# A linear-attention and MLP block on one core: layer-norm moments by a power on GpSimd, and five operand pairs prepared in the sweep

## The chip, the cores and the metric

The kernel runs on one core of a Trainium2 chip. The metric is the device time of one launch in microseconds (us). Three runs of the kernel before took 1133.1, 1133.49 and 1134.76 us, median 1133.49.

The engines are named as in the profile: PE is TensorE (PEld its weight loads), DVE is VectorE, ACT is ScalarE, POOL is GpSimd and SP the queue that issues DMAs. Each engine works through its own instructions in program order and waits for the others by semaphores.

## The reference

The input x has 2048 rows of 576 values. Two branches read it and a gate mixes them (shortened):

```python
qkv = (x @ wqkv)                        # 32 heads of 18
phi = lambda t: where(t > 0, t + 1, exp(t)) + 1e-6
kv  = einsum("bhsd,bhse->bhde", phi(k), v)
z   = phi(k).sum(over rows)
a   = (phi(q) @ kv) / (phi(q) @ z + 1e-6) @ wo

y = (x - mean(x)) / sqrt(var(x) + 1e-5)     # per row
b = gelu(y @ w1 + b1) @ w2 + b2             # 576 -> 4608 -> 576

g = sigmoid((x * gate_w).sum(-1))
out = g * a + (1 - g) * b
```

Everything is float32. To reach that accuracy a product is made of several matmuls over operands that are split into a rounded high part and the rest (a "split": ACT copies into the high part, DVE subtracts).

## The kernel before, in words

The 2048 rows are 16 tiles of 128. They are taken in pairs: `ORDER` lists the tiles so that neighbours in it form a pair, and `PLACE` is a tile's position in that list. Pairs 0 to 3 belong to the first half of the rows (`sup` 0), pairs 4 to 7 to the second.

**The sweep** (the loop `for n in range(FIRST, NT)`, after three tiles that are written out) visits each tile once. PE projects keys (`project(i, KEY, half)`, two halves of 14 matmuls), adds the first part of the products of the tile before (`add_products(before, 0)`), projects queries (two halves), and adds the second part. The projections use PSUM banks 6 and 7 in turn, so each half overwrites a bank that was read two halves earlier. The reader is `phi`: ACT makes e = exp of the negative part, then DVE combines it with the bank (`k<-ps,e` for keys, `accs<-ps,e` or `acc<-ps,e` for queries). DVE also makes the rest parts: `ks` of the keys, `xs` of the rows of x (twice, 512 and 64 wide), and `y<-t,y` of the next tile's transposed x (twice). POOL sums the keys over the tiles (`pks<-pks,k`). The last three tiles have no queries in the loop; these follow later.

**Jobs.** Into each tile of the sweep other work is put at three places, its thirds: `run(3 * n)` after the splits of keys and rows, `run(3 * n + 1)` after the queries' phi, `run(3 * n + 2)` after the second part of the products. `at(n, f, ...)` enters a job under its number. All jobs run in the program order of their engines; nothing is rescheduled.

**Moments and gates.** ACT takes each tile's sum of squares (`moments_of`) and copies the row sums out of the projection (`sums_of_x`). Groups of 2, 2, 4 and 8 tiles (`MOMENTS`) then go through `gates_in`, `gates_act` and `gates_out`: eleven DVE operations and, on ACT, an exponential and a square root, each with its own table of functions, which ACT reloads. `share_moments` transposes the group's means and inverse deviations by PE through bank 6, copies them out and stores them to DRAM as rows. The last group is done in the attention, after the sweep.

**Pairs for the MLP.** The MLP's first product uses a scheme with seven operands made of the four blocks of a pair (B11, B21, B12, B22) and four differences (T1 to T4; B12 has T1's place). `load_pair` loads `rows` (the pair's moments, spread over all partitions) and the transposed x into `yr`; `normal_pair` adds the negative mean and multiplies by the inverse deviation, once for each tile of the pair (4 operations, 768 wide); `sum_pair` makes the differences (4 operations, 384 wide); `split_pair` and `split_tails` split them in four parts (`ys`, the last in a place within `y`), and `store_pair` puts them to DRAM (`yd`). `rows` and `yr` lie in `spare`, a piece of the big tile `accs` (so does much else: in the profile "accs<-accs 128x768" are the additions and products of a pair and "accs<-accs 128x384" its differences). All of this is DVE's before, but for the copies of the splits. Pairs 0 to 3 are prepared in the sweep at hand-written thirds, pairs 4 to 7 in the first passes of the MLP, by `after(...)`.

**After the sweep** come the state kv and its product with `wo` (`xk`, `kvs`, `project_values`), the attention over 16 tiles, then the MLP from about 265 us to the end.

Of the kernel before, what the change touches and what calls it, by code (L numbers as in the profile page):

```python
# [33 lines left out]
MOMENTS = ((0, 2), (2, 4), (4, 8), (8, 16))  # L34
# [77 lines left out]
def tile_gated_mix(ctx: ExitStack, tc: tile.TileContext, x, xm, xe, wm, we, wvm, wve, wo, um, ue, w2, b1, b2, gw, out):  # L112
# [54 lines left out]
    nmean = keep.tile([P, NT], F32, name="nmean")  # L167
# [4 lines left out]
    mr = [keep.tile([P, 2, q1 - q0], F32, name=f"mr{b}") for b, (q0, q1) in enumerate(MOMENTS)]  # L172
    mt = keep.tile([P, 2, NT], F32, name="mt")
    mrt = keep.tile([2 * max(q1 - q0 for q0, q1 in MOMENTS), P], F32, name="mrt")
    moments = [dram.tile([2, (q1 - q0) * P], F32, name=f"moments{b}") for b, (q0, q1) in enumerate(MOMENTS)]
# [72 lines left out]

    def moments_of(i):
        own = slice(PLACE[i], PLACE[i] + 1)  # L250
        act.activation(xnraw[i], xnraw[i], AF.Square, bias=nmean[:, own], accum_out=sumsq[:, own])
# [30 lines left out]
    def sums_of_x(i):  # L282
        own = slice(PLACE[i], PLACE[i] + 1)
        act.activation(gsum[:, own], banks[i, KEY, 1][:, HALF:HALF + 1], AF.Copy)
        act.activation(nmean[:, own], banks[i, KEY, 1][:, HALF + 1:HALF + 2], AF.Copy, scale=-1 / D)
# [59 lines left out]
    def gate_parts(b):  # L345
        q0, q1 = MOMENTS[b]
        own, n = slice(q0, q1), q1 - q0
        return own, mt[:, 0, :n], mt[:, 1, :n], mr[b][:, 1]

    def gates_in(b):  # L350
        own, ve, _, _ = gate_parts(b)
        dve.tensor_copy(mr[b][:, 0], nmean[:, own])
        dve.tensor_scalar(ve, sumsq[:, own], 1 / D, EPS_LN, op0=OP.mult, op1=OP.add)

        dve.tensor_scalar(g[:, own], gsum[:, own], -87.0, None, op0=OP.max)

    def gates_act(b):
        own, ve, _, rstd = gate_parts(b)
        act.activation(g[:, own], g[:, own], AF.Exp, scale=-1.0)
        act.activation(rstd, ve, AF.Sqrt)  # L360
        if MOMENTS[b][1] < NT:
            act.activation(tiny, ones[:, 0:1], AF.Exp)

    def gates_out(b):
        own, ve, vr, rstd = gate_parts(b)
# [3 lines left out]
        dve.reciprocal(rstd, rstd)  # L369
# [19 lines left out]
    def load_pair(sup, j):  # L389
        q = sup * TPS + 2 * j  # L390
        b = [q0 <= q < q1 for q0, q1 in MOMENTS].index(True)
        c0 = (q - MOMENTS[b][0]) * P
        sp.dma_start(rows, moments[b][None, :, c0:c0 + 2 * P].to_broadcast([P, 2, 2 * P]))
        for a, m in enumerate((B11, B12)):
            i = ORDER[q + a]
            own = yr[:, m:m + 2]
            sp.dma_start(own[:, :, 0:2].rearrange("p h t n -> p h (t n)"), xm[i].rearrange("p (h n) -> p h n", h=2))
            for h in range(2):
                sp.dma_start(own[:, h, 2], four_times(xe[i], h))

    def normal_pair(sup, j, a, k):
        m = (B11, B12)[a]
        own = yr[:, m:m + 2].rearrange("p m s n -> p (m s) n")
        row = rows[:, k:k + 1, a * P:(a + 1) * P].to_broadcast([P, 6, P])
        dve.tensor_tensor(out=own, in0=own, in1=row, op=(OP.add, OP.mult)[k])

    def sum_pair(sup, j, n):
        to, x0, x1 = ((T3, B22, B12), (T1, B12, B11), (T2, B22, T1), (T4, B21, T2))[n]
        dve.tensor_tensor(out=yr[:, to], in0=yr[:, x0], in1=yr[:, x1], op=OP.subtract)
# [198 lines left out]
    ysc.close()  # L608
    a2 = ExitStack()
# [30 lines left out]
    xk = spare[:, :5 * D].rearrange("p (t n) -> p t n", n=D)  # L640
# [21 lines left out]
    project(late[1], QUERY, 1, n=0)  # L662
    kv = [ps[:GW, 1 + j // 3, j % 3 * GW:(j % 3 + 1) * GW] for j in range(G)]
# [252 lines left out]
    for j in range(4):  # L916
# [300 lines left out]
```

## Time and profile before

| | |
|---|---|
| runs | 1133.1, 1133.49, 1134.76 us |
| span of the profiled execution | 1130.0 us |
| the runs' median less that span | 3.5 us |
| PE busy | 1114.3 us, 99% |
| PEld, DVE, ACT, POOL busy | 90%, 76%, 49%, 27% |
| granted TensorE clock | 1.000 |

The profile holds one execution, with a span of 1130.0 us from its first to its last instruction; what lies around the span isn't in it, and the difference to the runs' median is the only measure of it here. All instructions have the line L108, since a helper (`InOrder`) issues them; they are told apart by tile and shape. In a row "out<-in" names the tiles, then come shapes and the count; a bracket at the end of a row of the time line is the engine's idle time before it, and what ended it.

### The profile page before, as it was taken

The page shows a single profiled execution, that of the slowest core. Times are in us where ns is not written, and L with a number is a line of the kernel's source. Part 1 is how long each engine was busy: PE and PEld are TensorE (multiplying, and loading weights), DVE is VectorE, ACT ScalarE, POOL GpSimd, SP SyncE. Part 2 cuts the span into 40 slices and gives each one's busy share as a digit, 9 for nine tenths or more (in the row PEclk, how much of TensorE's full clock was granted, in tenths as well). Part 3 has the DMA queues.
Part 4 walks back from the last instruction along what each step waited for, and adds up shares of the span by engine and source line. Part 5 has one row for each costly group of instructions (what it writes and reads, how often), then busy time and mean ns, then how long its engine had stood idle before and what let it go on. Part 6 is the DMA issues. An engine that isn't in the chain of part 4 may idle for free.

```text
span 1130.0 us, 18099 instructions
## 1 busy us (share of the span) xinstructions
PE 1114.3 (99%) x6871; PEld 1021.4 (90%) x6871; DVE 862.6 (76%) x1292; ACT 556.4 (49%) x953; POOL 303.3 (27%) x247
## 2 busy tenths in 40 slices
PE   8999899999999999999999999999999999999998
PEld 8999899999899999999999999989999999899988
DVE  4567675896569878779768775578898889888985
ACT  6667665453554544544444543364444444454441
POOL 1011112342111113112123111234353435343520
PEclk9999999999999999999999999999999999999999
DMA  6237555524554763654764549844444444444452
GB/s 177 63 113 259 164 174 186 201 94 161 182 169 142 250 223 137 232 168 168 240 212 154 210 142 388 308 121 131 126 127 136 126 126 128 136 124 126 131 180 84
DMA packets 102860, 189.84 MB, mean 168 GB/s; under 512 B 8159, under 2 KB 58623, under 8 KB 98550
## 3 DMA queue, kind: packets, MB, share of 16 engines
q1 hardware_dynamic: 102210, 188.10, 50.7%
q8 instruction: 54, 0.88, 0.3%
q10 hardware_dynamic: 564, 0.59, 0.2%
q14 instruction: 32, 0.26, 0.1%
HBM read 121.93 MB, written 66.73 MB: 167 GB/s over the span
## 4 chain that ended last, share of the span: by engine, by line
PE 89%; DVE 6%; ACT 2%; issue 1%; DMA 1%; SPq 0%; ACTq 0%; DVEq 0%
PE ps L108 89%; DVE den L108 1%; DVE accs L108 1%; DVE qt L108 1%; DVE region L108 1%; DVE u L108 0%; DVE acc L108 0%; DMA s<-in_wm 0%; DVE y L108 0%; DMA s<-in_we 0%; ACT L108 0%; SPq L108 0%; ACT h L108 0%; ACT u L108 0%; DVE wp L108 0%
## 5 line engine op out<-in xcount | busy, mean ns | idle before, releaser
L108 PEld LDWEIGHTS ps<-region,h 128*128 128x128 f32 x2568 | 368.5, 188 | 22.7 <-DVE accs L108 1.0
L108 PE MATMUL ps<-region,h 128*128 128x288 f32 x2568 | 383.1, 295 | 0.5 <-DVE region L108 0.2
L108 PE MATMUL ps<-y,wa 128*128 128x512 f32 x1008 | 265.0, 392 | 0.0
L108 POOL TENSOR_TENSOR fresh<-fresh 128x384 f32<-128x384 f32 (+1 forms) x128 | 137.8, 1081 | 439.5 <-DMA w1d<-wb 198.6
L108 PE MATMUL ps<-y,wb 128*128 128x512 f32 x756 | 200.9, 394 | 1.0 <-ACT u L108 1.0
L108 PEld LDWEIGHTS ps<-y,wa 128*128 128x128 f32 x1008 | 177.8, 188 | 26.2
L108 DVE TENSOR_TENSOR accs<-ps,accs 128x576 f32<-128x576 f32 x210 | 158.0, 753 | 33.2 <-PE ps L108 23.5
L108 ACT ACTIVATE h<-u,b1s 128x512 fp32r<-128x512 f32 x90 | 65.3, 725 | 214.8 <-DVE u L108 214.8
L108 PEld LDWEIGHTS ps<-y,wb 128*128 128x128 f32 x756 | 132.9, 188 | 23.0 <-ACT u L108 1.7
L108 DVE SCALAR_TENSOR_TENSOR accs<-ps,omg,accs 128x576 f32<-128x576 f32 (+1 forms) x146 | 118.0, 809 | 43.1 <-PE ps L108 42.3
L108 ACT ACTIVATE u<-ps 128x512 f32<-128x512 f32 x108 | 63.8, 591 | 149.9 <-PE ps L108 149.6
L108 POOL TENSOR_TENSOR u<-u 128x512 f32<-128x512 f32 x64 | 100.3, 1567 | 125.3 <-ACT u L108 121.6
L108 PE MATMUL ps<-y 128*128 128x288 f32 (+1 forms) x896 | 126.7, 298 | 1.1 <-ACT y L108 0.6
L108 PEld LDWEIGHTS ps<-y 128*128 128x128 f32 x896 | 123.5, 190 | 3.3 <-ACT y L108 1.2
L108 DVE TENSOR_TENSOR h<-u,h 128x512 fp32r<-128x512 f32 x142 | 104.8, 738 | 27.3 <-ACT u L108 27.1
L108 ACT ACTIVATE u<-u,b1s 128x512 f32<-128x512 f32 x108 | 78.2, 724 | 53.9 <-DVE u L108 50.9
L108 DVE TENSOR_TENSOR u<-ps,u 128x512 f32<-128x512 f32 x108 | 74.1, 686 | 36.6 <-ACT u L108 23.4
L108 PEld LDWEIGHTS ps<-region 128*128 128x128 f32 x600 | 90.3, 188 | 8.9 <-ACT accs L108 0.5
L108 DVE TENSOR_TENSOR region<-fresh,region 128x576 fp32r<-128x576 f32 (+1 forms) x83 | 81.2, 978 | 20.5 <-ACT region L108 20.5
L108 PE MATMUL ps<-region 128*128 128x288 f32 x600 | 96.2, 295 | 0.1
L108 PE MATMUL ps<-wp,qt 128*128 128x288 f32 x448 | 63.6, 298 | 0.8 <-DVE qt L108 0.8
L108 PEld LDWEIGHTS ps<-wp,qt 128*128 128x128 f32 x448 | 59.9, 188 | 1.3 <-DVE qt L108 1.3
(134 smaller groups left out, 1047.0 us busy)
## 6 DMA issues: line engine op xcount, KB each, us to landing
w1d<-wa SPq DMA_DIRECT2D x18, 1280.0 KB
wa<-w1d SPq DMA_DIRECT2D x72, 320.0 KB
y<-yd SPq DMA_DIRECT2D x14, 1280.0 KB
w1d<-wb SPq DMA_DIRECT2D x18, 960.0 KB
wb<-w1d SPq DMA_DIRECT2D x54, 320.0 KB
fresh<-in_w SPq DMA_DIRECT2D x20, 576.0 KB
fresh<-in_w SPq DMA_DIRECT2D x32, 288.0 KB
fresh<-in_um SPq DMA_DIRECT2D x64, 128.0 KB
```

The lines of the kernel that those rows point to most:

```text
L108: return lambda *args, **kwargs: self.tc.keep_in_program_order(op(*args, **kwargs))
```

## The change

- The mean (negative) is written by ACT straight into `mr`, a tile with the moments of all pairs; the inverse deviation is the power -0.5 of the variance, taken on POOL pair by pair (`scale_in`), followed by the same Newton step on DVE (`scale_out`).
- `share_moments` stores a pair's moments from `mr` without a transpose: 128 partitions x 4 single values.
- Gates keep only the sigmoid, in two groups of eight tiles, the second right after the sweep.
- Five pairs, not four, are prepared in the sweep, one every six thirds of a tile. In each, the additions of the mean and the four differences are POOL's; products and splits stay with DVE and ACT. `load_pair` issues `rows` last.
- The fifth pair is dropped from the MLP's first passes. `xk` gets a place of its own, and the list of jobs goes on behind the loop.

On POOL the sweep's order before, two tiles of a pair and more (`pks` is the sum of the keys):

```order
L108 TENSOR_TENSOR pks<-pks,k 128x576 x2
L108 MEMSET kvs 126x1152
L108 TENSOR_TENSOR pks<-pks,k 128x576 x13
L108 TENSOR_TENSOR qz<-accs,pks 128x576 x8
L108 TENSOR_TENSOR qz<-acc_87,pks 128x576
```

and after the change, from the third tile's sum on (`mr<-mt` is the power):

```order
L110 TENSOR_TENSOR pks<-pks,k 128x576
L110 TENSOR_TENSOR mr<-mt,minus_half 128x2
L110 TENSOR_TENSOR pks<-pks,k 128x576
L110 TENSOR_TENSOR accs<-accs 128x768 x2
L110 TENSOR_TENSOR accs<-accs 128x384 x4
L110 TENSOR_TENSOR pks<-pks,k 128x576
```

Between two sums of keys POOL now has, in every second tile, a pair's two additions and four differences.

On DVE, in the sweep, before: a pair's four additions and products, with the next tile behind them, where the differences begin.

```order
L108 TENSOR_TENSOR accs<-accs 128x768 x4
L108 SCALAR_TENSOR_TENSOR k<-ps,e 128x288
L108 TENSOR_TENSOR y<-t,y 128x512
L108 TENSOR_TENSOR y<-t,y 64x128
L108 SCALAR_TENSOR_TENSOR k<-ps,e 128x288
L108 SCALAR_TENSOR_TENSOR ks<-k,ks 128x576
L108 TENSOR_TENSOR xs<-xn,xs 128x512
L108 TENSOR_TENSOR xs<-xn,xs 128x64
L108 TENSOR_TENSOR accs<-accs 128x384 x2
L108 TENSOR_TENSOR ys_543<-accs,ys_543 128x2x256
```

After, the tile in which a pair is normalized:

```order
L110 SCALAR_TENSOR_TENSOR ks<-k,ks 128x576
L110 TENSOR_TENSOR xs<-xn,xs 128x512
L110 TENSOR_TENSOR xs<-xn,xs 128x64
L110 TENSOR_TENSOR y<-accs,y 128x256
L110 SCALAR_TENSOR_TENSOR y<-y,low_rows,accs 128x128
L110 SCALAR_TENSOR_TENSOR accs<-ps,e 128x288 x2
L110 TENSOR_TENSOR accs<-accs 128x768 x2
L110 TENSOR_TENSOR ys_544<-accs,ys_544 128x2x256
L110 SCALAR_TENSOR_TENSOR ys_544<-ys_544,low_rows,accs 128x2x128
L110 SCALAR_TENSOR_TENSOR k<-ps,e 128x288
```

Two 768-wide operations instead of four stand behind the phi of the queries (`accs<-ps,e`), and none of 384; the last split of the pair before (`y<-accs,y`, called T4 below) stands ahead of these phi.

The diff, cut to its core:

```diff
-    nmean = keep.tile([P, NT], F32, name="nmean")
+    mr = keep.tile([P, NP, 2, 2], F32, name="mr")
...
+    minus_half = keep.tile([P, 2], F32, name="minus_half")
+    dve.memset(minus_half, -0.5)
+    moments = [dram.tile([2, 2 * P], F32, name=f"moments{q}") for q in range(NP)]
...
     def gates_act(b):
-        own, ve, _, rstd = gate_parts(b)
+        own = slice(*GATES[b])
         act.activation(g[:, own], g[:, own], AF.Exp, scale=-1.0)
-        act.activation(rstd, ve, AF.Sqrt)
-        if MOMENTS[b][1] < NT:
-            act.activation(tiny, ones[:, 0:1], AF.Exp)
...
+    def scale_in(q):
+        ve = mt[:, 0]
+        dve.tensor_scalar(ve, sumsq[:, 2 * q:2 * q + 2], 1 / D, EPS_LN, op0=OP.mult, op1=OP.add)
+        pool.tensor_tensor(out=mr[:, q, 1], in0=ve, in1=minus_half, op=OP.pow)
+
+    def scale_out(q):
+        ve, vr, r = mt[:, 0], mt[:, 1], mr[:, q, 1]
 
-        dve.tensor_mul(vr, rstd, rstd)
+        dve.tensor_mul(vr, r, r)
         dve.tensor_mul(vr, vr, ve)
         dve.tensor_scalar(vr, vr, -0.5, 1.5, op0=OP.mult, op1=OP.add)
-        dve.tensor_mul(rstd, rstd, vr)
-
-    def share_moments(b, p):
-
-        n = 2 * (MOMENTS[b][1] - MOMENTS[b][0])
-        pe.transpose(p[:n], mr[b].rearrange("p a t -> p (a t)"), ident)
-        act.activation(mrt[:n], p[:n], AF.Copy)
-        sp.dma_start(moments[b].rearrange("a (t n) -> (a t) n", n=P), mrt[:n])
+        dve.tensor_mul(r, r, vr)
+
+    def share_moments(q):
+        sp.dma_start(moments[q].rearrange("a (t n) -> n a t", n=P), mr[:, q])
...
-    def normal_pair(sup, j, a, k):
+    def normal_pair(sup, j, a, k, by=dve):
...
-    def sum_pair(sup, j, n):
+    def sum_pair(sup, j, n, by=dve):
...
-    for b, (n, shared) in enumerate(((9, 13), (13, 16), (24, 28))):
-        at(n, gates_in, b)
-        at(n + 1, gates_act, b)
-        at(n + 2, gates_out, b)
-        at(shared, share_moments, b, ps[:, 6, :P])
-
-    for j, (loaded, *parts) in enumerate(((13, 18, 19, 20, 21), (20, 25, 27, 28, 29), (28, 33, 34, 35, 36),
-                                          (35, 41, 42, 44, 45))):
...
+    def prepare_scale(q, n):
+        at(n, scale_in, q)
+        at(n + 1, scale_out, q)
+        at(n + 2, share_moments, q)
+
+    for q in range(PAIRS_IN_SWEEP):
+        sup, j = divmod(q, TPB)
+        n = 6 * q
+        prepare_scale(q, max(n + 7, 3 * FIRST))
+        at(n + 13, load_pair, sup, j)
         for a in range(2):
-            for k in range(2):
-                at(loaded + 3 + a, normal_pair, 0, j, a, k)
+            at(n + 15, normal_pair, sup, j, a, 0, pool)
+            at(n + 16, normal_pair, sup, j, a, 1)
         for m in range(4):
-            at(parts[m // 2], sum_pair, 0, j, m)
...
+            at(n + 17, sum_pair, sup, j, m, pool)
+        for part in range(4):
+            at(n + (17, 19, 20, 21)[part], split_pair, sup, j, part, lambda part=part: y_stages[part])
+            at(n + (17, 19, 20, 21)[part], split_tails, sup, j, part)
+            at(n + (20, 22, 23, 24)[part], store_pair, sup, j, part)
+    prepare_scale(5, 37)
+    prepare_scale(6, 44)
+    for n, f in ((49, gates_in), (50, gates_act), (51, gates_out)):
+        at(n, f, 1)
+    prepare_scale(NP - 1, 50)
...
-    xk = spare[:, :5 * D].rearrange("p (t n) -> p t n", n=D)
+    xk = xkp.tile([P, 5, D], F32, name="xk")
...
-    for i, part in ((1, gates_in), (2, gates_act), (3, gates_out)):
-        extra[i] += [lambda part=part: part(len(MOMENTS) - 1)]
-    extra[5] += [lambda: share_moments(len(MOMENTS) - 1, two_of(t_pairs)[:, 0, :P])]
...
-    for j in range(4):
+    for j in range(PAIRS_IN_SWEEP - TPB, TPB):
         k, s = divmod(15 + 28 * j, TPS)
```

More of the change, by code (lines that the diff above doesn't have):

```diff
@@ L33 @@
 PLACE = [ORDER.index(i) for i in range(NT)]
-MOMENTS = ((0, 2), (2, 4), (4, 8), (8, 16))
+NP = NT // 2
+GATES = ((0, 8), (8, 16))
+PAIRS_IN_SWEEP = 5
 EPS_PHI = 1e-6
@@ L171, in tile_gated_mix @@
     omg = keep.tile([P, NT], F32, name="omg")
[L172 to L175, printed above, removed]
+    mt = keep.tile([P, 2, 2], F32, name="mt")
+    minus_half = keep.tile([P, 2], F32, name="minus_half")
+    dve.memset(minus_half, -0.5)
+    moments = [dram.tile([2, 2 * P], F32, name=f"moments{q}") for q in range(NP)]
     w1d = [dram.tile([P, 7, 5, P], F32, name=f"w1d{c}") for c in range(NCHUNK)]
@@ L247, in load_xn, with nmean_of @@
         sp.dma_start(xnraw[i], x[i * P:(i + 1) * P, :])
+    def nmean_of(i):
+        q, a = divmod(PLACE[i], 2)
+        return mr[:, q, 0, a:a + 1]
     def moments_of(i):
         own = slice(PLACE[i], PLACE[i] + 1)
-        act.activation(xnraw[i], xnraw[i], AF.Square, bias=nmean[:, own], accum_out=sumsq[:, own])
+        act.activation(xnraw[i], xnraw[i], AF.Square, bias=nmean_of(i), accum_out=sumsq[:, own])
     halves_in, banks = cycle((6, 7)), {}
@@ L284, in sums_of_x @@
         act.activation(gsum[:, own], banks[i, KEY, 1][:, HALF:HALF + 1], AF.Copy)
-        act.activation(nmean[:, own], banks[i, KEY, 1][:, HALF + 1:HALF + 2], AF.Copy, scale=-1 / D)
+        act.activation(nmean_of(i), banks[i, KEY, 1][:, HALF + 1:HALF + 2], AF.Copy, scale=-1 / D)
     def sum_keys(i):
@@ L343, in add_products @@
                 pe.matmul(to, a, b, start=opens and i == ORDER[0], stop=i == ORDER[-1], skip_group_check=True)
[L345 to L348, printed above, removed]
     def gates_in(b):
-        own, ve, _, _ = gate_parts(b)
-        dve.tensor_copy(mr[b][:, 0], nmean[:, own])
-        dve.tensor_scalar(ve, sumsq[:, own], 1 / D, EPS_LN, op0=OP.mult, op1=OP.add)
+        own = slice(*GATES[b])
         dve.tensor_scalar(g[:, own], gsum[:, own], -87.0, None, op0=OP.max)
     def gates_act(b):
-        own, ve, _, rstd = gate_parts(b)
+        own = slice(*GATES[b])
         act.activation(g[:, own], g[:, own], AF.Exp, scale=-1.0)
-        act.activation(rstd, ve, AF.Sqrt)
-        if MOMENTS[b][1] < NT:
-            act.activation(tiny, ones[:, 0:1], AF.Exp)
     def gates_out(b):
-        own, ve, vr, rstd = gate_parts(b)
+        own = slice(*GATES[b])
         dve.tensor_scalar(g[:, own], g[:, own], 1.0, None, op0=OP.add)
@@ L390, in load_pair @@
         q = sup * TPS + 2 * j
-        b = [q0 <= q < q1 for q0, q1 in MOMENTS].index(True)
-        c0 = (q - MOMENTS[b][0]) * P
-        sp.dma_start(rows, moments[b][None, :, c0:c0 + 2 * P].to_broadcast([P, 2, 2 * P]))
         for a, m in enumerate((B11, B12)):
@@ L399, in load_pair @@
                 sp.dma_start(own[:, h, 2], four_times(xe[i], h))
-    def normal_pair(sup, j, a, k):
+        sp.dma_start(rows, moments[q // 2][None].to_broadcast([P, 2, 2 * P]))
+    def normal_pair(sup, j, a, k, by=dve):
         m = (B11, B12)[a]
@@ L404, in normal_pair @@
         row = rows[:, k:k + 1, a * P:(a + 1) * P].to_broadcast([P, 6, P])
-        dve.tensor_tensor(out=own, in0=own, in1=row, op=(OP.add, OP.mult)[k])
-    def sum_pair(sup, j, n):
+        by.tensor_tensor(out=own, in0=own, in1=row, op=(OP.add, OP.mult)[k])
+    def sum_pair(sup, j, n, by=dve):
         to, x0, x1 = ((T3, B22, B12), (T1, B12, B11), (T2, B22, T1), (T4, B21, T2))[n]
-        dve.tensor_tensor(out=yr[:, to], in0=yr[:, x0], in1=yr[:, x1], op=OP.subtract)
+        by.tensor_tensor(out=yr[:, to], in0=yr[:, x0], in1=yr[:, x1], op=OP.subtract)
     ys = {}
@@ L531, in tile_gated_mix @@
     y_stages.append(y_place.rearrange("p (m s n) -> p m s n", m=2, s=5))
-    jobs = {n: [] for n in range(3 * NT)}
+    jobs = {n: [] for n in range(3 * NT + 9)}
     def at(n, f, *args):
@@ L601, in tile_gated_mix @@
     moments_of(end)
+    run(48)
     for part in range(2):
         add_products(end, part)
+    run(49)
     pz = [ps[:, 6 + half, :HALF] for half in range(2)]
@@ L662, in tile_gated_mix @@
     project(late[1], QUERY, 1, n=0)
+    run(50)
     kv = [ps[:GW, 1 + j // 3, j % 3 * GW:(j % 3 + 1) * GW] for j in range(G)]
@@ L668, in tile_gated_mix @@
     queries_out(late[1])
+    run(51)
     for i in range(1, 3):
@@ L704, in tile_gated_mix @@
         project_values(t)
+        run(52 + t)
         if t < 4:
```

13 lines of the change are left out of this document (5 added, 8 removed).

## The prediction, made before the result was known

> **What bounds the kernel now.** I read the page first, then the busy time by stretch, then the time line of the sweep, because almost everything that the change moves lies in the sweep (about 20 to 185 us).
>
> ```profile
> span 1130.0 us, 18099 instructions
> PE 1114.3 (99%) x6871; PEld 1021.4 (90%) x6871; DVE 862.6 (76%) x1292; ACT 556.4 (49%) x953; POOL 303.3 (27%) x247
> ```
>
> TensorE (PE) is the bound: it is idle for 15.7 us in all. The three runs have a median of 1133.49 us, 3.5 us over this span; I keep that distance and count changes of the span. The stretches tell where PE is idle (each row: length, then the busy us of PE, PEld, DVE, ACT, POOL).
>
> ```profile
> 50.00:75.00 25.00, 23.80 (x159) 22.55 (x158) 14.17 (x40) 18.95 (x43) 2.87 (x2) 1.00 0.29 81
> 100.00:125.00 25.00, 22.02 (x146) 20.57 (x145) 18.17 (x43) 17.56 (x40) 2.87 (x2) 1.00 0.45 146
> 125.00:150.00 25.00, 25.00 (x170) 24.07 (x169) 18.93 (x34) 16.26 (x37) 2.88 (x2) 1.00 0.61 194
> 210.00:265.00 55.00, 53.41 (x407) 52.20 (x406) 51.02 (x91) 26.24 (x58) 20.11 (x15) 1.00 0.54 200
> 300.00:725.00 425.00, 425.00 (x2575) 388.01 (x2574) 319.88 (x424) 196.60 (x262) 84.90 (x68) 1.00 0.61 210
> ```
>
> From 300 to 725 us PE never stops, so that a pair less for the VectorE (DVE) there can give nothing. What can be won is 25.00 - 23.80 = 1.20, 25.00 - 22.02 = 2.98 and 55.00 - 53.41 = 1.59 us. The first two are the transposes of the moments, as the time line shows, and part of the third is:
>
> ```profile
> 73.02 0.27 PE L108 MATMUL ps<-accs,mr 128*4 128x128 f32 x1 [1.20 <-DVE accs L108]
> 121.35 0.27 PE L108 MATMUL ps<-accs,mr 128*8 128x128 f32 x1 [2.78 <-DVE acc L108]
> 237.83 0.66 PE L108 MATMUL ps<-accs 128*128 128x128 f32 x4 [0.65 <-DVE qt L108]
> ```
>
> The transpose borrows bank 6, so PE stands until DVE has finished the phi (`queries_out`) that reads this bank, and DVE is late there because of the gates' small operations.
>
> **What the change removes.** Four transposes with these waits, four copies out of PSUM, seven reloads of ScalarE's (ACT's) function tables, and in the attention, where DVE is busy for 51.02 of 55 us, eleven small DVE operations.
>
> ```profile
> L108 ACT ACT_TABLE_LOAD x9 | 11.5, 1283 | 4.4 <-DMA t<-in_xm 4.4
> L108 DVE TENSOR_TENSOR mr<-mr,mt x4: 160/162/168, 52.7 to 232.5; 128x2 f32<-128x2 f32 x2, 128x4 f32<-128x4 f32 x1, 128x8 f32<-128x8 f32 x1
> L108 SPq DMA_DIRECT2D moments<-mrt x4: 276/317/340, 61.6 to 238.3; - x4
> ```
>
> ACT is no bound (49%), so its 7 x 1.28 us by themselves are worth nothing. Eleven operations of 0.16 us are 1.8 us of DVE in the attention; PE's idle 1.59 us there can shrink by most of it, I take 1.4. Sum won: 1.20 + 2.98 + 1.4 = **5.6 us**; bounds 4.2 (the transposes alone) and 5.8.
>
> **What it adds at no cost.** Eight powers of 128x2 on GpSimd (POOL): the trace has no power. Below, nothing; above, an operation of POOL's longest shape here (2.8 us, quoted below), which the lighter tile of each two could still carry (its room is worked out below): zero. The eight stores of moments have 512 runs of 4 bytes instead of 4 to 16 rows; the queue's issue was 0.32 us, at most a few times that. Nothing waits for it for four thirds of a tile, so I count zero. The second gate group and the last power land between 185 and 195 us, some nine small operations (1.5 us); the product kvs at 195.57 (quoted below with the tile) is preceded by 1.92 us of idle DVE. Zero too.
>
> **What it moves, and the lock.** Per pair, two of four 768-wide operations and all four 384-wide ones go from DVE to POOL:
>
> ```profile
> L108 DVE TENSOR_TENSOR accs<-accs 128x768 f32<-128x768 f32 x16 | 15.1, 953 | 0.3
> L108 DVE TENSOR_TENSOR accs<-accs 128x384 f32<-128x384 f32 x16 | 8.8, 553 | 0.3
> L108 POOL TENSOR_TENSOR accs<-accs 128x384 f32<-128x384 f32 x8 | 8.8, 1113 | 10.4 <-DMA accs<-in_ue 6.3 <-DMA b2b<-in_b 3.8
> L108 POOL TENSOR_TENSOR accs<-accs 128x1152 f32<-128x1152 f32 x3 | 8.4, 2803 | 20.6 <-DVE accs L108 20.6
> ```
>
> DVE is freed of 2 x 0.95 + 4 x 0.55 = 4.1 us. On POOL a 384-wide one takes 1.0 to 1.1 us and a 768-wide one, halfway to 1152, some 1.9: 2 x 1.9 + 4 x 1.05 = 8 us per pair. POOL has the time (2.9 of 25 us busy). But DVE and POOL shut each other out. Two rows of each engine:
>
> ```profile
> 20.77 0.76 DVE L108 SCALAR_TENSOR_TENSOR ks<-k,ks 128x576 fp32r<-128x576 f32 x1
> 20.98 1.86 POOL L108 TENSOR_TENSOR pks<-pks,k 128x576 f32<-128x576 f32 x1 [2.90 <-DVE k L108]
> 21.67 0.46 DVE L108 SCALAR_TENSOR_TENSOR k<-ps,e 128x288 f32<-128x288 f32 x1
> 129.03 1.44 POOL L108 TENSOR_TENSOR pks<-pks,k 128x576 f32<-128x576 f32 x1 [11.51 <-DVE k L108]
> 129.85 1.24 DVE L108 SCALAR_TENSOR_TENSOR ks<-k,ks 128x576 fp32r<-128x576 f32 x1 [0.96 <-ACT ks L108]
> ```
>
> At 20.77 DVE began first: its ks took 0.76 us and POOL's sum was stretched from 1.44 to 1.86. At 129.85 POOL was first and DVE took 1.24: 129.85 + 1.24 - 0.76 = 130.33, so it began work 0.14 us before POOL's end at 130.47. That is a wait for the whole instruction of the other, not a sharing. The phi, with one operand in PSUM, takes 0.46 us under POOL's sum at 21.67 as it does alone at 131.92 (below), so only DVE operations with two SBUF operands are shut out. The Trainium skill (SBUF — State Buffer, "SBUF: two separate sides") has the same: a port pair of DVE and GpSimd held by whoever started first for the whole instruction. The trace agrees, 1.24 against 0.76 us. Neither says who goes next when POOL waits and DVE has a second such operation right behind the first; on that the sign hangs.
>
> Now one undisturbed tile of the sweep, with the deadlines of PE:
>
> ```profile
> 131.01 0.81 DVE L108 TENSOR_TENSOR xs<-xn,xs 128x512 fp32r<-128x512 f32 x2
> 131.92 0.46 DVE L108 SCALAR_TENSOR_TENSOR acc<-ps,e 128x288 f32<-128x288 f32 x1
> 133.77 0.46 DVE L108 SCALAR_TENSOR_TENSOR acc<-ps,e 128x288 f32<-128x288 f32 x1 [1.39 <-ACT e L108]
> 134.65 3.90 PE L108 MATMUL ps<-y 128*128 128x288 f32 x28
> 137.87 0.45 DVE L108 SCALAR_TENSOR_TENSOR k<-ps,e 128x288 f32<-128x288 f32 x1
> 140.14 3.87 PE L108 MATMUL ps<-y 128*128 128x288 f32 x28
> 145.85 3.90 PE L108 MATMUL ps<-y 128*128 128x288 f32 x28
> 157.05 3.90 PE L108 MATMUL ps<-y 128*128 128x288 f32 x28
> 172.01 3.90 PE L108 MATMUL ps<-y 128*128 128x288 f32 x28
> 195.57 0.81 DVE L108 TENSOR_TENSOR kvs<-ps,accs 126x126 f32<-126x126 f32 x5 [1.92 <-PE ps L108]
> ```
>
> A tile is 145.85 - 134.65 = 11.2 us of PE. The next tile's keys at 134.65 overwrite the bank of the first query half, so the phi of 131.92 must be over by then; its slack is 134.65 - 132.38 = 2.3 us. The phi of 137.87 has until 140.14.
>
> In the new order POOL has, behind the sum of the keys (pks), the two additions of a pair at once; DVE has ks, xs twice, the last piece of the pair before (T4), the two phi, the two products. Other durations needed:
>
> ```profile
> L108 DVE TENSOR_TENSOR xs<-xn,xs 128x512 fp32r<-128x512 f32 x16 | 10.9, 681 | 0.1
> L108 DVE TENSOR_TENSOR xs<-xn,xs 128x64 fp32r<-128x64 f32 x16 | 3.4, 212 | 0.0
> L108 DVE TENSOR_TENSOR y<-accs,y 128x256 fp32r<-128x256 f32 x4 | 1.7, 413 | 0.0
> L108 DVE SCALAR_TENSOR_TENSOR y<-y,low_rows,accs 128x128 fp32r<-128x128 f32 x4 | 1.4, 340 | 0.0
> L108 DVE TENSOR_TENSOR ys<-accs,ys 128x512 fp32r<-128x512 f32 x12 | 8.2, 686 | 3.0 <-ACT ys L108 3.0
> L108 DVE SCALAR_TENSOR_TENSOR ys<-ys,low_rows,accs 128x256 fp32r<-128x256 f32 x12 | 5.7, 479 | 0.0
> L108 DVE TENSOR_TENSOR y<-t,y 128x512 fp32r<-128x512 f32 x13 | 9.0, 691 | 1.1 <-ACT y L108 0.2
> L108 DVE TENSOR_TENSOR y<-t,y 64x128 fp32r<-64x128 f32 x13 | 3.8, 289 | 0.4
> ```
>
> If the two engines take turns: ks ends at 131.09; POOL's first addition follows, to 132.9; xs 132.76 to 133.44; the second addition to 135.2; the short xs 135.06 to 135.27; T4 0.41 + 0.34, to 136.0; phi 136.0 to 136.45. PE starts its keys at 136.45 instead of 134.65: 1.8 us lost. Behind it the four subtractions on POOL take turns with ys, its tail and the two y, and the phi of the second key half comes another 0.2 us late. **2.0 us a pair** for pairs 1 to 3. A check from the sums: DVE's own work in this tile is 0.76 + 0.89 + 0.75 + 0.92 + 1.9 + 1.17 + 0.92 + 0.98 = 8.3 us, its waits 0.5 (pks) + 2 x 1.76 (additions) + about 3 (subtractions, 4 x 0.91 less what the phi cover), together 15.3. The other tile of each two has two splits (2.3) and five small operations (0.8) in place of T4, products and ys, 7.6 us, 8.1 with the wait for pks, so 3.1 us of room. 15.3 + 8.1 - 22.4 = 1.0 us cannot be made good however the slack is used: the lower bound of a pair. The upper one, when `rows` lands some 3 us late and the products wait for it, is 2.7. Pair 0 has no T4 before it: 136.45 - 0.75 - 134.65 = 1.05. Pair 4 falls into the last tiles, which have no queries and last half of 172.01 - 157.05 = 14.96, 7.5 us each; the same waits there push the split of the last tile's x behind the keys at 172.01, where I get 3.0 us (bounds 1.7 and 4). Sum lost: 1.05 + 3 x 2.0 + 3.0 = **10.0 us**; bounds 1.05 + 3 x 1.0 + 1.7 = 5.8 and 1.05 + 3 x 2.7 + 4 = 13.2.
>
> Taking turns it is 10.0 - 5.6 = +4.4 us: 1133.5 + 4.4 = **1138**. Its own range is 1133.5 + 5.8 - 5.8 = 1133.5 to 1133.5 + 13.2 - 4.2 = 1142.
>
> **Rivals.** (1) DVE keeps the port while it has operations queued. Then xs, xs and T4 run on behind ks to 132.7, the additions overlap both phi, the first product starts at 134.5 and the second, behind the second addition, at 137.2; the phi of the keys ends at 139.9, before 140.14. No stall is left, the 5.6 us are won whole: 1128. For it: DVE's operations follow each other without a gap (0.68 + 0.21 took 0.81 us at 131.01), which leaves POOL little time to get in. Against it: nowhere in the trace does POOL wait at such a pair, so nothing shows it. (2) Mixed: POOL gets in at some of the borders, and half of the 10 us is lost: 5.0 - 5.6, that is 1133, no change. (3) The change doesn't win what its removals promise, because PE's waits at 73 and 121 us come from DVE's lateness and return at the next matmul of bank 6, while turns are taken: of the 4.2 us some 2 return, 1140. Speaks against it that DVE loses the gates' operations too. Taking turns costs from the point at which POOL holds the port for more than 2.3 us between ks and the first phi; (1) decides as soon as the second xs goes ahead of POOL's second addition.
>
> **How the numbers follow.** Turns 0.44, DVE keeps the port 0.33, mixed 0.18, waits that return 0.05. A measurement of this kernel tells a change from none at about 0.2%, 2.3 us. Of the turns' 0.44 some 0.04 lies at their lower bound, within it. Slower: 0.40 + 0.05 = 0.45; within: 0.18 + 0.04 = 0.22; faster: 0.33. Predicted time 1138, that of the likeliest. The range from 1127 (all of 5.8 us and a little) to 1142 holds the turns with their bounds and the other cases.
>
> **What would show it.** The phi of the queries, in tiles with the additions, ends 3 to 4 us after its matmuls instead of 1.4; PE's idle time before the keys names DVE, about 2 us every second tile from 70 to 165 us, and PE is busy for 23 of 25 us there; POOL's additions take 1.9 us, more where DVE was first; xs takes about 1.8 us from its start. Wrong it is if PE is busy for 25 of 25 us in these stretches, or if POOL's additions are stretched to 3 us and xs isn't: then DVE kept the port, and the time is 1128.

## The result, and the profile after

The changed kernel takes 1141.05 us (median of four runs, 1139.73 to 1142.28) against 1133.3 us before on the same chip: 1.0066 times as long, 95% interval 1.0052 to 1.0080. It is slower by 7.5 us (5.9 to 9.1), as forecast in sign; the forecast size was 4.4.

The head of the page after, and the stretches (length, busy us of PE, PEld, DVE, ACT, POOL, then clock, DMA share, GB/s):

```profile
span 1138.3 us, 18127 instructions
PE 1116.6 (98%) x6867; PEld 1023.5 (90%) x6867; DVE 866.7 (76%) x1267; ACT 545.7 (48%) x933; POOL 354.9 (31%) x285
50.00:75.00 25.00, 25.00 (x170) 24.06 (x169) 14.95 (x30) 12.79 (x31) 7.22 (x5) 1.00 0.52 105
75.00:100.00 25.00, 23.68 (x160) 22.46 (x159) 22.13 (x36) 16.16 (x38) 13.96 (x10) 1.00 0.64 183
100.00:125.00 25.00, 25.00 (x166) 23.62 (x164) 18.91 (x36) 13.86 (x33) 12.53 (x11) 1.00 0.92 236
125.00:150.00 25.00, 18.23 (x111) 17.54 (x111) 14.27 (x27) 14.76 (x34) 9.84 (x8) 0.86 0.84 186
150.00:192.00 42.00, 38.36 (x242) 35.32 (x241) 37.13 (x59) 24.79 (x58) 23.00 (x17) 1.00 0.80 182
217.00:272.00 55.00, 54.49 (x420) 53.93 (x419) 48.98 (x81) 25.98 (x58) 20.89 (x16) 1.00 0.61 236
```

The gains are there: PE is busy for 25.00 us at 50 and at 100 us, where it lost 1.20 and 2.98, and its idle time in the attention went from 1.59 to 0.51. The losses are there too, in three places; the one at 125 us, 25.00 - 18.23 = 6.77 us, isn't in the prediction. The time line of PE (start, length, what, and in brackets the wait) names its waits in the sweep; two short ones near 184 us are left out:

```profile
97.00 4.00 PE L110 MATMUL ps<-y 128*128 128x288 f32 x28 [1.31 <-DVE accs L110]
131.93 6.03 PE L110 MATMUL ps<-y 128*128 128x288 f32 x28 [6.77 <-DVE k L110]
152.49 4.01 PE L110 MATMUL ps<-y 128*128 128x288 f32 x28 [1.32 <-DVE acc L110]
180.19 1.30 PE L110 MATMUL ps<-y 128*128 128x288 f32 x8 [1.28 <-ACT mr L110]
...
```

Two kinds of wait stand here. **The lock** is at 97, 152 and 180 us. The time line at 91 us shows it on both engines:

```profile
90.72 1.23 DVE L110 SCALAR_TENSOR_TENSOR ks<-k,ks 128x576 fp32r<-128x576 f32 x1 [0.96 <-ACT ks L110]
91.61 4.29 POOL L110 TENSOR_TENSOR accs<-accs 128x768 f32<-128x768 f32 x2 [0.28 <-DMA accs<-moments]
91.87 4.11 DVE L110 TENSOR_TENSOR xs<-xn,xs 128x512 fp32r<-128x512 f32 x2
...
96.50 0.81 DVE L110 SCALAR_TENSOR_TENSOR accs<-ps,e 128x288 f32<-128x288 f32 x2
```

The two xs need 4.11 us in place of 0.81. The prediction had them from 131.09 to 135.27 for taking turns, 4.18 us.

**A late store** is at 131.93. Ahead of the late phi, DVE and ACT stand at a split; ACT's row in the time line:

```profile
129.55 0.84 ACT L110 ACTIVATE ys<-accs 128x768 fp32r<-128x768 f32 x1 [10.95 <-DMA yd<-ys]
```

The split of a pair's operands needs its stage `ys`, from which the pair before is still being stored; ACT stands for 10.95 us, the phi of the keys is queued behind this split on DVE, and PE waits for that. In the new table a stage is used again three thirds of a tile after its store is issued; before it was five to seven. What SP issued there, the store of that stage at 114.49 among it:

```profile
112.66 0.43 SPq L110 DMA_DIRECT2D wv<-in_wvm  x1
113.14 1.30 SPq L110 DMA_DIRECT2D wv<-in_wve  x2
114.49 0.64 SPq L110 DMA_DIRECT2D yd<-ys  x1
...
122.49 0.38 SPq L110 DMA_DIRECT2D moments<-mr  x1
```

And the view of the DMA engines from 123 to 130 us (40 slices of 0.175 us: busy tenths, then the rate), after the change:

```profile
DMA  7699589989999909921698275095261996849999
GB/s 285 247 222 204 142 244 399 358 299 271 188 88 102 44 0 29 15 29 35 61 102 44 44 29 28 0 29 28 29 59 44 132 117 59 102 72 145 217 202 220
DMA packets 940, 0.87 MB, mean 124 GB/s; under 512 B 552, under 2 KB 599, under 8 KB 940
```

The store stands behind the load of wv, 1.3 MB, which the change issues two thirds of a tile later than before, right ahead of it (`load_wv` moves from `3 * 8` to `3 * 8 + 2`, a line that the shortened diff leaves out). And while the moments' 512 runs of 4 bytes go out (most of the 552 packets under 512 B) and after them, from about 125 to 129 us, the engines are counted busy for more than half of the time and yet never move more than 132 GB/s. The same follows the store of moments at 147.13 us: 0.65 MB from 149 to 156 us. The store lands when ACT is released, at 129.5: 15.0 us after its issue. The wait also costs afterwards: the granted clock was 0.86 in this stretch, and the 28 matmuls behind it took 6.03 us where they take 4.00 behind the waits of 1.3. The Trainium skill (TensorE: Matmul & The Clock Gate, Part 1) says the clock is halved after an idle window of about 3.4 us; the trace agrees for this wait, with 6.03 against 4.00 us, though another run has the same behind a wait of 1.78 us (the last section).

### The profile page after: what moved, and what is told of

The parts are those of the page before. It is cut to its first block, busy times and chain, and to the rows that moved or that the text cites. A ratio compares the mean times of both kernels' runs of the same rounds, so it can differ in the third digit from the quotient of the medians.

```text
span 1138.3 us, 18127 instructions
## 1 busy us (share of the span) xinstructions
PE 1116.6 (98%) x6867; PEld 1023.5 (90%) x6867; DVE 866.7 (76%) x1267; ACT 545.7 (48%) x933; POOL 354.9 (31%) x285
## 4 chain that ended last, share of the span: by engine, by line
PE 81%; DMA 7%; DVE 6%; issue 2%; ACT 2%; SPq 1%; POOL 0%; ACTq 0%; DVEq 0%
PE ps L110 81%; DMA yd<-ys 3%; DMA t<-in_xm 1%; SPq L110 1%; DVE accs L110 1%; DMA accs<-in_xe 1%; DMA wv<-in_wve 1%; DVE den L110 1%; DVE xs L110 1%; DVE region L110 1%; DVE y L110 0%; DVE u L110 0%; POOL accs L110 0%; DVE qt L110 0%; DVE ys L110 0%
## 5 line engine op out<-in xcount | busy, mean ns | idle before, releaser
L110 PEld LDWEIGHTS ps<-y,wb 128*128 128x128 f32 x756 | 133.0, 188 | 23.1 <-ACT u L110 1.7
L110 PE MATMUL ps<-y 128*128 128x288 f32 (+1 forms) x896 | 129.3, 302 | 12.2 <-DVE k L110 6.8
L110 DVE TENSOR_TENSOR region<-fresh,region 128x576 fp32r<-128x576 f32 (+1 forms) x83 | 84.0, 1012 | 22.5 <-ACT region L110 22.5
L110 POOL TENSOR_TENSOR accs<-accs 128x384 f32<-128x384 f32 (+2 forms) x41 | 61.8, 1513 | 50.2 <-DVE accs L110 24.2
```

Of the source, the lines that this page charges most:

```text
L110: return lambda *args, **kwargs: self.tc.keep_in_program_order(op(*args, **kwargs))
```

## The experiments

Theories: A, the 4-byte stores; B, the load of wv ahead of the store; C, the early reuse of the stage; L, the lock (DVE and POOL taking turns); M, in place of L, the load of five pairs on DVE. The results, each against the kernel before on the same chip:

| moments | additions, differences | wv | pairs | median us | ratio, 95% interval |
|---|---|---|---|---|---|
| 512 x 4 B (the change) | POOL | early | 5 | 1141.05 | 1.0066, 1.0052 to 1.0080 |
| 128 x 16 B | POOL | early | 5 | 1136.16 | 1.0026, 1.0014 to 1.0039 |
| 512 x 4 B | DVE | early | 5 | 1140.58 | 1.0067, 1.0043 to 1.0091 |
| 128 x 16 B | DVE | early | 5 | 1129.73 | 0.9972, 0.9959 to 0.9984 |
| 512 x 4 B | POOL | later | 5 | 1137.56 | 1.0036, 1.0023 to 1.0049 |
| 128 x 16 B | POOL | later | 5 | 1133.17 | 1.0002, 0.9993 to 1.0011 |
| 128 x 16 B | DVE | later | 5 | 1127.89 | 0.9958, 0.9945 to 0.9972 |
| transposes, bank 7 | DVE | later | 4 | 1126.96 | 0.9951, 0.9937 to 0.9964 |

Differences below are ratios times 1133 us; each is uncertain by about 2 us, by 3 where the third row takes part. In the rows with 128 x 16 B the moments lie in DRAM in another order than the pairs read them in: these kernels leave out the right order and serve for the time alone.

### Runs of 16 bytes

```diff
-        sp.dma_start(moments[q].rearrange("a (t n) -> n a t", n=P), mr[:, q])
+        flat = moments[q].rearrange("a n -> (a n)").rearrange("(n m) -> n m", m=4)
+        sp.dma_start(flat, mr[:, q].rearrange("n a t -> n (a t)"))
```

> The changed kernel, with each pair's moments stored as 128 runs of 16 bytes in place of 512 runs of 4 bytes. The rows of moments in DRAM then come in another order, so the MLP half normalizes with the wrong values; amount of data, instructions and their order are the same. It takes away the 4-byte runs alone. Theory A (the 4-byte stores hold up the packets behind them, so that the store of a split comes late, the next split of that part waits, and PE stands 6.8 us at 124.8 us and gets a clock of 0.86 behind that): no packet near the stores takes over 1 us, the stall is gone, the time is 1141.05 - 6.9 - 2 = 1132. Rival B (the load of wv, put directly ahead of that store, makes it late) and rival C (a split's stage is used again after three thirds of a tile in place of six, whatever the queue carries): the stall stays, 1139 to 1141.

Measured: 1136.16 us, about half of the gain that theory A said. The ten runs lie between 1133.77 and 1138.86 us, and the profile is of one that took 1138.38: it shows the wait of a long run. The DMA engines from 123 to 130 us run again:

```profile
DMA packets 1217, 2.00 MB, mean 286 GB/s; under 512 B 258, under 2 KB 430, under 8 KB 1217
```

PE's wait is shorter, but there, and the chain of waits has the same store ahead of it:

```profile
130.01 6.49 PE L110 MATMUL ps<-y 128*128 128x288 f32 x28 [3.56 <-DVE k L110]
```

```profile
114.59 11.95 DMA yd<-ys
```

The same 7 us carry 2.00 MB in place of 0.87. So the 4-byte runs are a cause worth 7.5 - 2.9 = 4.6 us by the medians, and not the only one: the store issued at 114.59, behind wv, still lands 11.95 us after it, in place of 15.0.

### Additions and differences on DVE, alone and with 16 bytes

```diff
-            at(n + 15, normal_pair, sup, j, a, 0, pool)
+            at(n + 15, normal_pair, sup, j, a, 0)
...
-            at(n + 17, sum_pair, sup, j, m, pool)
+            at(n + 17, sum_pair, sup, j, m)
```

> The changed kernel, with a pair's two additions and four differences on VectorE again (512 runs of 4 bytes as in the change). Theory L (VectorE and GpSimd take turns at the shared port, which costs 1.5 us in pairs 1 and 3 and 2.8 us in pair 4): xs takes 0.81 us in every tile, PE's waits of 1.3 us behind the phi go, the time is 1141.05 - 5.8 = 1135, with the stall at 124.8 us left as it is. Rival M (the price is VectorE's load: five pairs in fewer tiles, each 4.1 us of VectorE more than in the change): the waits behind the phi stay or grow to 2 us a pair, 1141 to 1144.

> Both edits: moments in 128 runs of 16 bytes (in another order, so the MLP half normalizes with the wrong values) and the additions and differences on VectorE. If theories A and L are both right and independent, what is left is what the change removed: 1133.3 - 5.6 = 1127.7, or 1141.05 - 8.9 - 5.8 = 1126.4. With A alone right 1132, with L alone right 1135, with rival M in place of L 1132 to 1135.

Measured: 1140.58 alone, and 1129.73 with 16 bytes. The same edit is worth nothing beside the 4-byte runs and 6.1 us without them. The first run's PE shows where the 6 us went:

```profile
121.40 4.01 PE L110 MATMUL ps<-y 128*128 128x288 f32 x28 [1.70 <-DVE acc L110]
135.38 5.60 PE L110 MATMUL ps<-y 128*128 128x288 f32 x28 [8.21 <-DVE k L110]
181.93 3.98 PE L110 MATMUL ps<-y 128*128 128x288 f32 x28 [1.19 <-DVE k L110]
```

The waits of 1.3 us at the lock are gone; PE comes sooner to a store that doesn't land sooner (ACT is released at 133.0, in the change at 129.5), and waits 8.21 us in place of 6.77; the 1.70 us before it is the additions, now ahead of the phi on DVE, whose rows came late. With 16 bytes the late store is still there, but shorter: it lands 10.80 us after its issue, in the first run 16.48; ACT waits for it for 5.61 us and PE for 1.42 (the chain of waits, then ACT's row in the time line):

```profile
112.70 10.80 DMA yd<-ys
123.61 0.85 ACT L110 ACTIVATE ys<-accs 128x768 fp32r<-128x768 f32 x1 [5.61 <-DMA yd<-ys]
```

Rival M isn't needed: with the stores in time (below) five pairs on DVE leave one wait, of 1.19 us.

### wv later

```diff
-    at(3 * 8 + 2, load_wv)
+    at(3 * 11 + 1, load_wv)
```

> The changed kernel, with the load of wv (1.3 MB) moved eight thirds of a tile later, from just ahead of the store of a split to behind it. Rival B (this load makes the store late): the stall at 124.8 us is gone, 1141.05 - 6.9 - 2 = 1132. Theory A (the 4-byte stores): packets behind the stores take as long as in the change, the stall stays or shrinks by a part, 1138 to 1141. If the load and the 4-byte stores make the store late only together, 1132 here and 1132 with runs of 16 bytes too.

Measured: 1137.56, 3.4 us less than the change. The wait at 125 us shrinks and another appears, behind stores that follow 4-byte runs and now wv too (PE's time line):

```profile
127.08 2.12 PE L110 MATMUL ps<-y 128*128 128x288 f32 x14 [1.24 <-DVE k L110]
...
177.44 5.57 PE L110 MATMUL ps<-y 128*128 128x288 f32 x28 [4.76 <-ACT mr L110]
```

In the chain of waits ahead of the second stands a store that took 16.28 us:

```profile
144.09 16.28 DMA yd<-ys
```

Neither A nor B alone: the two add up, 3.4 and 4.6 us, 7.3 taken away together (below).

### 16 bytes and wv later, with either engine

> The changed kernel with moments in runs of 16 bytes (in another order, so the MLP half normalizes with the wrong values), additions and differences on VectorE, and wv loaded eight thirds of a tile later. Beside the run without the last edit (1129.73): if wv ahead of the store makes the stall of 1.58 us at 124 us, it goes and the time is 1128. If the early reuse of the stage does, it stays: 1129.7. If wv only moves the lateness to the next store, a stall appears at 160 to 172 us instead: 1129.7 or more.

> The same with the additions and differences on GpSimd as in the change (moments in runs of 16 bytes, in another order, wv later). It is the lock alone: beside the run with them on VectorE the difference is what taking turns costs. Theory L, from the waits of 0.88, 1.49, 1.48 and 1.46 + 0.83 + 0.53 us that stand in the trace of the run with 16-byte runs: 6.7 us, so 1128 + 6.7 = 1134.5 to 1135. By the prediction's sum of 10.0 us: 1138. If most of what looked like the lock were late transfers: 1128 to 1131.

Measured: 1127.89 with DVE, 1133.17 with POOL. No late store is left in either; the wait of 1.42 us of the run with wv early is gone. PE's waits in its time line, with POOL (rows like the second, 1.34 and 1.32, and two of pair 4, 0.67 and 0.36, are left out):

```profile
74.57 4.01 PE L110 MATMUL ps<-y 128*128 128x288 f32 x28 [0.72 <-DVE accs L110]
98.57 4.00 PE L110 MATMUL ps<-y 128*128 128x288 f32 x28 [1.32 <-DVE accs L110]
...
174.26 1.30 PE L110 MATMUL ps<-y 128*128 128x288 f32 x8 [1.28 <-ACT mr L110]
```

and with DVE, where this is the only one:

```profile
169.50 3.97 PE L110 MATMUL ps<-y 128*128 128x288 f32 x28 [1.19 <-DVE k L110]
```

For this one the chain of waits names no store; ahead of it stand the fifth pair's additions, products and differences on DVE. The two runs show the lock by itself: a wait in every pair, and a difference of 0.2 + 4.8 = 5.0 us. Theory C falls as a cause of its own: with the stores in time the early reuse of the stage costs nothing. That it is what makes a late store matter was not tried apart.

### Transposes into columns that no projection uses

```diff
-        at(shared, share_moments, b, ps[:, 6, :P])
+        at(shared, share_moments, b, ps[:, 6, 3 * P:])
```

> The kernel before, with one edit: the transposes of the moments write columns 384 to 512 of bank 6, which no projection uses, in place of columns 0 to 128; everything else as before. My account of what the change removes says that PE stood at 73 and 121 us only because the transpose overwrote what the phi still had to read. Then these waits (1.20 and 2.98 us) go and nothing takes their place: 1132.7 - 4.2 = 1128.5. The rival: VectorE is late there anyway, and PE waits for the same phi at the next keys in bank 6; half or more of the 4.2 us returns, 1130.5 to 1132.7.

Measured: 1132.7 against 1133.19, a ratio of 1.0 (0.9991 to 1.0009). It did not test what it should: in PE's time line the transpose still waits for the phi,

```profile
121.63 0.27 PE L108 MATMUL ps<-accs,mr 128*8 128x128 f32 x1 [2.80 <-DVE acc L108]
```

so the wait that the program keeps goes by the bank, whichever columns are written. It leaves the rival open.

### A transpose per pair, in place of scattered stores

The change with additions on DVE, wv later, and for each pair but the last:

```diff
-        sp.dma_start(moments[q].rearrange("a (t n) -> n a t", n=P), mr[:, q])
+        p = ps[:4, 6, 3 * P:]
+        pe.transpose(p, mr[:, q].rearrange("p a t -> p (a t)"), ident)
+        act.activation(mrt, p, AF.Copy)
+        sp.dma_start(moments[q].rearrange("a (t n) -> (a t) n", n=P), mrt)
```

> The changed kernel's power, five pairs and two gate groups, but a pair's moments go through a transpose of 4 columns into the free columns of bank 6 and a store of 4 rows of 512 bytes (the last pair, after the sweep, keeps the scattered store), additions and differences are VectorE's, and wv is loaded eight thirds of a tile later. If the jam, the lock and the load of wv are the whole price, this is the run with 16-byte runs and both on VectorE (1129.7), less its last stall of 1.6 us, plus seven transposes of 0.27 us: 1130. If a split's stage that comes back after three thirds of a tile is a limit by itself, a stall of 1.5 to 5 us stays near 125 or 172 us: 1131.5 to 1135.

Measured: 1145.5, ratio 1.0116 (1.0100 to 1.0131), the slowest but one, by the bank again. The queries behind the transpose wait until ACT has copied it, and ACT has the splits to do first; and the seventh pair's transpose waits for DVE in the last tiles (PE's time line):

```profile
95.15 3.97 PE L110 MATMUL ps<-y 128*128 128x288 f32 x28 [1.78 <-ACT mrt L110]
190.33 0.37 PE L110 MATMUL ps<-accs,mr 128*4 128x128 f32 x1 [5.31 <-DVE mr L110]
```

### Rows read with a stride, five pairs and four

16-byte runs need no transpose if the additions read every fourth value of the rows (shown for five pairs; the second run has `PAIRS_IN_SWEEP = 4` and the fifth pair's moments prepared at its old place):

```diff
-        row = rows[:, k:k + 1, a * P:(a + 1) * P].to_broadcast([P, 6, P])
+        row = rows.rearrange("p k n -> p (k n)").rearrange("p (n k a) -> p k a n", k=2, a=2)
+        row = row[:, k, a:a + 1].to_broadcast([P, 6, P])
```

> The kernel with runs of 16 bytes, additions and differences on VectorE and wv later (1127.89), made right: the rows of moments lie in DRAM and in the tile on all partitions as 128 groups of four values, and the additions and products read every fourth value. If such a read takes VectorE as long as a dense one (0.94 us for 768 elements), the time stays at 1128. If it takes twice as long, each pair costs 4 x 0.94 us of VectorE more in a tile that has 1 us to spare: about 2.5 us a pair, 1140.

> The same with four pairs in the sweep and the fifth back in the MLP's first passes, as in the kernel before. In the run with five, the stall of 1.35 us at 168 us is the fifth pair's (its differences on VectorE in the sweep's last tiles): it goes, and the first passes, where TensorE never waits, carry the pair as they did before: 1128 - 1.35 = 1126.6. If a pair less for VectorE in the MLP is worth something, 1128 or more.

Measured: 1143.83 (ratio 1.0092, 1.0078 to 1.0106) and 1140.53 (1.0066, 1.0054 to 1.0079). DVE's groups (count, then busy us and mean ns), of the run with 16 bytes, DVE and wv later, which reads dense rows:

```profile
L110 DVE TENSOR_TENSOR accs<-accs 128x768 f32<-128x768 f32 x32 | 29.7, 954 | 0.0
```

and of this one with five pairs:

```profile
L110 DVE TENSOR_TENSOR accs<-accs 128x768 f32<-128x768 f32 x32 | 48.9, 1558 | 0.0
```

A step of 16 bytes in one operand makes 1.63 times of 0.954 us, 2.4 us more in each pair's tile, and cost 15.2 us in all (1.0092 against 0.9958). The Trainium skill (SBUF — State Buffer, "Door 1: The DMA port swizzle") speaks of 16-byte lines and a penalty for each access that goes to a new line, which fits the 1558 ns. My 1126.6 for four pairs went by dense reads; what can be read from the pair of runs is 2.9 us for the fifth pair.

### Rows later, with POOL

```diff
-        at(n + 13, load_pair, sup, j)
+        at(n + 13, load_pair, sup, j, False)
+        at(n + 15, load_rows, q)
```

> The kernel with runs of 16 bytes and wv later, additions and differences on GpSimd (1133.17; moments in another order, so the MLP half normalizes with the wrong values), with the load of a pair's rows issued two thirds of a tile later, behind the stores of the pair before. GpSimd's two additions then start some 3 us later, behind the two xs and the T4 piece of VectorE. If the lock costs only because the two engines take turns at exactly that place, xs takes 0.81 us again, PE's waits of 0.9 and 1.5 us at the keys go in pairs 0 to 3 (5.4 us), and the time is 1128 to 1129.5. If GpSimd's slower additions and differences are the price (8 us a pair in place of 4.1), the products come late, the wait moves to the keys' second half or to the splits, and the time stays at 1133 or more.

Measured: 1149.51 (ratio 1.0152, 1.0128 to 1.0175), both expectations wrong. The delay overshot: the rows are issued at 94.84 and the additions start at 103.09, in place of 92.85 with the rows early. The time line of pair 1:

```profile
94.96 0.81 DVE L110 TENSOR_TENSOR xs<-xn,xs 128x512 fp32r<-128x512 f32 x2
...
103.09 3.59 POOL L110 TENSOR_TENSOR accs<-accs 128x768 f32<-128x768 f32 x2 [8.67 <-DMA accs<-moments]
...
104.95 3.41 DVE L110 TENSOR_TENSOR accs<-accs 128x768 f32<-128x768 f32 x2 [6.76 <-POOL accs L110]
```

xs is undisturbed (0.81), as taking turns has it; the products now stand at the head of DVE for 6.76 us with the keys' phi behind them, and PE waits 6.40 us for that. A smaller delay is in the run with 16 bytes and wv early, by chance: in its pair 2 the rows came late, and PE's next keys (120.79) began without a wait. Its time line:

```profile
117.16 0.81 DVE L110 TENSOR_TENSOR xs<-xn,xs 128x512 fp32r<-128x512 f32 x2
...
119.24 3.65 POOL L110 TENSOR_TENSOR accs<-accs 128x768 f32<-128x768 f32 x2 [2.62 <-DMA accs<-moments]
120.79 3.90 PE L110 MATMUL ps<-y 128*128 128x288 f32 x28
```

With the additions 2.62 us behind the sum of the keys the lock costs nothing at the next keys, and with them right behind it, 1.3 us: in these tiles it is the meeting with xs and T4 that costs, not POOL's slower work.

### Dense rows, both causes removed

From the run with a transpose per pair: bank 7 and the head of its third, so that ACT's copy has a half of the queries' time; pairs 6 and 7 together in the attention; four pairs in the sweep.

```diff
+    def share_moments(q0, q1, p):
+        n = 4 * (q1 - q0)
+        pe.transpose(p[:n], mr[:, q0:q1].rearrange("p q a t -> p (q a t)"), ident)
+        act.activation(mrt[:n], p[:n], AF.Copy)
+        for q in range(q0, q1):
+            sp.dma_start(moments[q].rearrange("a (t n) -> (a t) n", n=P), mrt[4 * (q - q0):4 * (q - q0) + 4])
...
+        if q < 6:
+            jobs[n + 2].insert(0, lambda: share_moments(q, q + 1, ps[:, 7, :P]))
...
+    prepare_scale(4, 31)
...
+    extra[5] += [lambda: share_moments(6, 8, two_of(t_pairs)[:, 0, :P])]
```

> What the runs point to, with dense rows: the changed kernel's power on GpSimd and two gate groups, additions and differences on VectorE, four pairs in the sweep, wv eight thirds later, and the moments of pairs 0 to 5 through a transpose of 4 columns each into bank 7 (not 6), between the first part of the products and the queries, so that the next matmuls into that bank come 1.95 us later; pairs 6 and 7 go together, by a transpose of 8 columns in the attention. All stores of moments are rows of 512 bytes and all reads of them dense. From the run with runs of 16 bytes, VectorE and wv later (1127.89): less the stall of 1.35 us of the fifth pair, plus seven transposes of 0.27 us: 1128.4. If ScalarE's copy out of bank 7 is not over within 1.95 us of the transpose, each of the pairs holds up the second half of the queries by up to 1.8 us, as the transposes into bank 6 did for the first half: 1133 to 1137.

Measured: 1126.96 us against 1132.0, ratio 0.9951 (0.9937 to 0.9964): 5 us faster than the kernel before and the lowest median of all, though within the noise of the run with 16 bytes, DVE and wv later (0.9958). PE has no wait left in the sweep; the stretches:

```profile
100.00:125.00 25.00, 25.00 (x165) 23.23 (x163) 21.81 (x48) 17.13 (x42) 3.57 (x3) 1.00 0.71 254
125.00:150.00 25.00, 25.00 (x167) 23.27 (x166) 20.93 (x43) 16.12 (x38) 4.36 (x4) 1.00 0.74 239
150.00:192.00 42.00, 42.00 (x279) 39.59 (x278) 24.18 (x55) 24.20 (x59) 11.79 (x10) 1.00 0.44 158
```

## Why the prediction was right in sign and short in size

The three edits can be taken off one after the other, from the change at 7.5 us above the kernel before: 4-byte runs (to 2.9), wv (to 0.2), POOL (to -4.8). What is left is what the change wins.

| step | predicted us | measured us |
|---|---|---|
| won: transposes and small operations | -5.6 | -4.8 |
| lock on DVE and POOL | +10.0 | +5.0 |
| moments' stores | 0 | +4.6 |
| wv, two thirds later | not named | +2.7 |
| sum | +4.4 | +7.5 |

What the prediction summed, the win and the lock, measures -4.8 + 5.0 = +0.2 us: with POOL in place and the stores in time the kernel takes as long as before (1.0002, 0.9993 to 1.0011). The 4.4 us that it forecast are not there. The change is slower because of the moments' stores and wv, 7.3 us, which stood in the sum at zero or not at all. So the right sign, and a time within the range, are partly luck: a lock priced 5.0 us too high stood in for them.

- **Won, 5.6.** Right within the uncertainty, though 0.20 of the 2.98 us is another wait, at 114.59, behind the phi of the keys and not a transpose. The waits at the transposes go for good; the third rival (they return at bank 6) falls, since PE is busy for 25.00 of 25 us in the last run. Whether the transposes or the gates' operations ahead of the phi made them, no run tells apart.
- **No cost of the powers and gates.** Right: POOL takes 0.70 to 1.07 us for a power, and PE's waits name none of it.
- **Turns.** The mechanism is right, with the signs that were named (two xs of 4.11 us, PE waiting for DVE every second tile), so the first rival, DVE keeping the port, falls, and the mixed one too: POOL gets in at every border. The sum was too large. In the run with POOL and the stores in time, PE's waits at the keys are 0.72 in pair 0 (1.05 predicted), 1.32 to 1.34 in pairs 1 to 3 (2.0), and 1.28, 0.67 and 0.36 in pair 4 (3.0): together 7.0 of 10.0. The pair term of 2.0 was mis-sized: 1.3 stands for the 1.8 at the first phi, and nothing for the 0.2 at the second half of the keys. The same pairs on DVE also leave a wait, 1.19 us in the last tiles, which the prediction had not set against the lock: 7.0 - 1.2 = 5.8 is the measured 5.0 within its uncertainty. In the change itself pairs 0 and 2 show no such wait, so PE is busy for 25 of 25 us at 50 and 100 us, which the prediction had named as a sign of being wrong: their rows came late, and POOL's additions began 1.11 and 2.58 us behind the sum of the keys, which took xs out of their way in pair 2 and in part in pair 0.
- **The stores, zero: the step that failed.** "Nothing waits for it for four thirds of a tile" asked only who waits for the moments. Their issue was 0.38 us, as costed. But the runs slow whatever shares the DMA engines with them: the store of a stage that ACT needs, issued 8 us ahead of them, lands 15.0 us after its issue, and 11.95 with 16 bytes. Worth 4.6 us.
- **wv was left out.** The diff moves `load_wv` by two thirds, past the store of a split; the prediction counted no price for a moved transfer of 1.3 MB. Worth 2.7 us.
- **The terms don't add in any order.** The lock is worth 0 beside the 4-byte runs, 6.1 without them and 5.0 with wv later too.

## What to carry to other kernels

Price a transfer by what shares the DMA engines with it, not only by who reads it: list for each moved or scattered DMA the stores and loads in flight around it and when their buffers are needed again. When a change has several costs, take each away in the presence and in the absence of the others, since a wait pinned to a transfer's landing swallows every gain ahead of it. Work for GpSimd that shares a port with VectorE is best let in where VectorE reads PSUM or is idle; which instruction it meets sets its price: in the change a phi took 0.46 us at 118.63 under POOL's additions, and xs 4.11 in place of 0.81.

## What the runs showed of the hardware

- 512 runs of 4 bytes to DRAM slow the transfers around and behind them to at most 132 GB/s for about 4 us; 128 runs of 16 bytes with the same content don't (0.87 against 2.00 MB in the same 7 us). The Trainium skill (DMA: Bandwidth & Descriptors, "Why small descriptors are slow (HBM only)") has a fixed cost for each small descriptor; here the cost fell on other transfers in flight. What in the memory or the engines makes it so, no run tells.
- DVE and POOL take turns even within two DVE operations that follow each other without a gap: 0.81 us became 4.11, against two additions.
- One DVE operand read in steps of 16 bytes: 1.558 us in place of 0.954.
- Behind waits of PE of 3.56 to 8.21 us, 28 matmuls took 5.57 to 6.60 us. Behind waits up to 1.78 us they took 3.97 to 4.01, but for one: in the run with a transpose per pair one wait of 1.78 us, at 119.70, was followed by 5.50 us, at a granted clock of 0.73, while other waits of 1.78 us in the same run were followed by 3.97 and 3.98. Between, it varied too: with rows later they took 5.51 behind 2.20, and behind the wait of 2.8 in the kernel before and with free columns the granted clock of the stretch was 1.00 and 0.95. What decides between them, no run tells.
